# Two of the seven up products made of seven again, with the blocks of x reloaded from DRAM

## The chip, the cores and the metric

The kernel runs on one core of one Trainium2 chip, in one launch. The time is that of the device for one execution, in microseconds (us); the number given for a kernel is the median of its runs. The profile is one further execution, taken by the hardware profiler: it lists the instructions of each engine (PE multiplies matrices, PEld loads its weights, DVE and ACT are the vector and the scalar engine, POOL is GpSimd, SP issues DMAs), when each ran, and what released it when it had waited.

## The reference

An attention without softmax (features from exponentials of a projection) is computed for 8 batches, 8 heads, 576 tokens, 64 wide; its output, as 4608 tokens of 512, goes through a mixture of eight experts, whose shares P come from eight rounds of row and column scaling:

```python
x = np.ascontiguousarray(attn_out.transpose(0, 2, 1, 3)).reshape(B * S, H * D)   # 4608 x 512
...
for e in range(E):                       # E = 8
    h = np.maximum(x @ w1[e], 0.0)       # "up":   512 -> 1024
    ye = h @ w2[e]                       # "down": 1024 -> 512
    out += P[:, e:e + 1] * ye
```

All eight experts are computed for all tokens, so the two matmuls of the loop are most of the work. The inputs come from one fixed draw.

## The kernel before, in words

**Tiles.** x is held transposed in SBUF as bf16, `xT` of 128 partitions x 4 chunks x 4608 tokens. Tokens go in nine groups of 512; groups 0 to 7 are taken in four pairs (1024 tokens), group 8 alone. The results are summed up in fp32 in `acc`, one tile for each group.

**Seven products for eight.** For experts 1 to 7 both matmuls use Winograd's form of Strassen's scheme: each operand is cut into 2 x 2 blocks, sums of blocks are made, and seven block products take the place of eight. The blocks of w1 are added by `sums_up` (L1223), those of w2 by `sums_down` (L1248), those of h inside `down7` (L1468), all on DVE in bf16. The blocks of x are added once, by `sums_x` in expert 1 (L1299): one sum, t1, stands in `xT` in place of a block, three (t2, t3, t4) are stored to DRAM (`Xd`) and loaded again by every later expert (`load_x`, L1317) into the ring `X` of four buffers.

**One unit of work.** `up7` (L1343) makes the seven products of a quarter of the hidden width for a pair: each for two halves q of 128 hidden columns (one PSUM bank each), each half two matmuls of 512 columns (`wide`, L1334, profile line L1338): 28 wide matmuls. The products are called x1, y1, w1, x2, x3, x4, w2. The second (y1, blocks 12 and 21) and the fifth (w1, blocks s1 and t1) are the ones that the change speaks of. What is to be added to two outputs is copied by ACT: x1's bank is copied into y's banks (`move`, L1387) so that y1 accumulates on top of it, x2's into z's, and w1's result goes to SBUF (`keep`, `U`, L1383). Results go to `hs` in bf16 through a Relu, on ACT (`relu`, L1395) where one bank holds the whole sum, or on DVE where the part in `U` has to be added first (`add`, L1390, the ADD_SAT operation that the profile calls CUSTOM_DVE_ANT_0). `down7` makes seven products of one group from such h: 56 matmuls of 256 columns (`product`, L1323, profile line L1329); its results reach `acc` over DVE (`read`, L1522) or over ACT and POOL (`read2`, L1534).

**Loops.** For each expert, for each pair (group 8 last, in expert 7 first), for both quarters fp: one `up7` unit and, interleaved with it, one `down7` of a group whose h is finished. A pair gives two units, group 8 one: nine an expert, in experts 1 to 7. Expert 0 is computed plainly, in and after the attention.

**What sets the order.** Each operation is put into a `Plan` with an engine, an assumed length, what it reads and writes, and buffers. `Plan.schedule` (L261) then plays all engines forward with these lengths: each engine takes the operation that can start first, and among equals the one given first. Each engine's instructions are put out in that order and carry semaphore waits for what they read. The string `ORDER` (L1593) gives the order in which the steps of an up unit (x10 is x1 for half 0) and of a down product set (X1 to Z2) are handed over. Loads of x are issued on SP's queue in the planned order ("order of X"), weights on POOL's. PSUM's eight banks are given out by the class `Banks` (L70): "P1" any bank, "PO" only a bank that a whole-bank matmul started before, since what ACT copies into it is then accumulated on.

Of the kernel before, what the change touches and what calls it, by code (L numbers as in the profile page):

```python
# [17 lines left out]
class Buf:  # L18


    def __init__(self, ring):
        self.ring, self.t, self.slot, self.left, self.end = ring, None, None, 0, 0.0
        self.last = None

# [174 lines left out]
class Plan:  # L199
# [3 lines left out]
    def __init__(self):  # L203
        self.last, self.readers = {}, {}
        self.ops = []
        self.prio = 0
        self.port, self.vector = 0.0, None

    def op(self, eng, dur, lat, fn, r=(), w=(), takes=(), nbytes=0, shared=False):
# [19 lines left out]
        o.bufs = list({id(b): b for b in bufs}.values())  # L229
        for b in o.bufs:  # L230
            b.left += 1
# [12 lines left out]
    def start(self, o, free):  # L244

        t = max(free, o.ready, self.port if o.shared else 0.0)
        if o.eng == "POOL" and o.shared and self.vector:
            t = max(t, self.vector.end)
        need = {}
        for b in o.bufs:  # L250
            if b.slot is None:
                n = need[b.ring] = need.get(b.ring, 0) + 1
                at = b.ring.find(n)
                if at is None:
                    return None
                t = max(t, at)
            elif b.last is not None and b.last.eng != o.eng:
                t = max(t, b.last.end)
        return t

    def schedule(self):  # L261
# [22 lines left out]
        while len(done) < len(self.ops) or links.next():  # L284
# [18 lines left out]
            for b in o.bufs:  # L303
                if b.slot is None:
                    b.slot = b.ring.take(at)
            dur = clock.takes(at, o.dur, o.tiled) if o.eng == "PE" else o.dur
            free[o.eng] = at + dur
# [28 lines left out]
def kernel(  # L336
# [11 lines left out]
    nc = tc.nc  # L348
# [132 lines left out]
    banks = {i: 0.0 for i in range(8)}  # L481
    whole = set()
    for tag, n, kind in (("P1", 1, "whole"), ("P2", 2, "part"), ("PP", 1, "part"),
# [739 lines left out]
    def sums_up(e, w1):  # L1223
# [13 lines left out]
        def k(a):  # L1237
            return [(w1, *a)]
# [4 lines left out]
        sub(dve, 1024, s(3), q(*a12), s(1), ALU.subtract, k(a12) + [S[1]] + late, [S[3]])  # L1243
        return {"11": (q(*a11), k(a11)), "12": (q(*a12), k(a12)), "22": (q(*a22), k(a22)),
                "s1": (q(*a21), k(a21)), "s2": (s(1), [S[1]]), "s3": (s(2), [S[2]]),
                "s4": (s(3), [S[3]])}

# [33 lines left out]
    def xall(gs):  # L1281
        return [k for g in gs for k in xkeys(g)]

    Xd = {(g, n): dram.tile([128, 2, 2, 256], BF16, name=f"xd{g}{n}")
          for g in range(0, NG, 2) for n in (2, 3, 4)}
# [13 lines left out]
    def sums_x(gs, r0=()):  # L1299
# [13 lines left out]
        for n in (3, 2, 4):  # L1313
            move_x(gs, n, True, X)
        return X

# [26 lines left out]
    def up7(A, gs, fp, X, H, r0, inner=()):  # L1343
# [3 lines left out]

        def b(n):
            f, r = {"11": (xq(gs, 0, 1), []), "21": (xq(gs, 1, 1), []), "22": (xq(gs, 1, 0), []),
                    "t1": (xq(gs, 0, 0), []),  # L1350
                    "t2": (lambda: X[2](), [X[2]]), "t3": (lambda: X[3](), [X[3]]),
                    "t4": (lambda: X[4](), [X[4]])}[n]
            return f, r

# [6 lines left out]
        def prod(bank, q, x, y, first, more=(), takes=(), wk=()):  # L1361
            f, r = A[x]
            rhs, r2 = b(y)
            r = xall(gs) + r + r2 + list(more)
            if pair:
# [35 lines left out]
        more = [("banks", i, q) for i in range(2) for q in range(2)]  # L1401
        more += [k for n in ("s2", "s3", "22") for k in A[n][1]] + [X[2]] + list(r0)

# [24 lines left out]
        def w2(q):  # L1428
# [4 lines left out]
            ("x1", x1), ("y1", y1), ("x2", x2), ("w1", w1), ("x3", x3), ("x4", x4), ("w2", w2))  # L1433
            for q in range(2)}

    def acc_part(g, i, j):
# [179 lines left out]
    early, dn = [plain(8)], plain(7)  # L1616
    pairs = [(g, g + 1) for g in range(0, 8, 2)]
    for e in range(1, E):
# [4 lines left out]
        B7 = sums_down(e, w2) if e > 1 else None  # L1623
        turn = [*pairs, (8,)] if e < E - 1 else [(8,), *pairs]
        for n, gs in enumerate(turn):
            X = nextX if e == 1 else load_x(gs)
            H = {g: [] for g in gs}
            for fp in range(len(gs)):
                hs = take()
                for i, z in enumerate(hs):  # L1630
                    H[gs[min(i, len(gs) - 1)]].append(z)
                un = up7(A7, gs, fp, X, H, ["up0"])
                for o in EARLY if e == 1 else ORDER:
                    if len(o) == 3:
# [48 lines left out]
```

## Time and profile before

| | us |
|---|---|
| median of 3 runs | 1022.17 (1021.77 to 1022.48) |
| span of the profiled execution, first to last instruction | 1020.4 |
| what lies around that span, against the median | 1.8 |
| PE busy | 1006.6 |
| DVE busy | 777.5 |
| ACT busy | 743.5 |
| POOL busy | 379.5 |

The profile gives the span and not a time of its own for that execution; the 1.8 us are the difference to the median. A row of a group reads: line, engine, operation, output<-inputs, shapes, count | busy us, mean ns of one | idle time before them and what ended it. Busy time joins rows that overlap. A row of the order in time reads: start, length from the first start to the last end, engine, line, operation, count, and in brackets the idle time ahead of it and its releaser. A matmul's row contains the way of its last result out of the array, so a following matmul starts before it ends; PE's pace is read from starts.

### The profile page before, as it was taken

How to read it: one execution, taken by the hardware profiler on the slowest of the kernel's cores; microseconds unless marked ns; L12 is line 12 of the kernel's file. 1: busy time of each engine (PE TensorE's matmuls, PEld its weight loads, DVE VectorE, ACT ScalarE, POOL GpSimd, SP SyncE). 2: the span in 40 equal slices, each digit the busy share in tenths (PEclk: the TensorE clock that was granted, in tenths of full speed). 3: DMA queues.
4: the chain of work that ended last, by engine and by line, in shares of the span. 5: the costliest groups of instructions: out<-in, count | busy, mean ns of one | idle time of the engine just before them, and what ended most of it. 6: DMA issues, size and time to landing. Idle time of an engine off the chain costs nothing.

```text
span 1020.4 us, 21307 instructions
## 1 busy us (share of the span) xinstructions
PE 1006.6 (99%) x7944; PEld 685.8 (67%) x7944; DVE 777.5 (76%) x1707; ACT 743.5 (73%) x1594; POOL 379.5 (37%) x418
## 2 busy tenths in 40 slices
PE   7899999999999999999999999999999999999998
PEld 5666666644666766676667766676667666776665
DVE  7999989986877777777678767777667767777665
ACT  7999999836988766667666666666666666666663
POOL 5778764400134233322224333422232323333222
PEclk9999999999999999999999999999999999999999
DMA  9999978160013311161116111421125110613333
GB/s 256 181 192 178 183 133 131 38 114 11 32 42 66 86 32 32 27 134 32 31 28 115 31 41 37 80 57 31 32 46 116 32 32 26 119 33 73 133 123 127
DMA packets 107015, 82.85 MB, mean 81 GB/s; under 512 B 53536, under 2 KB 89376, under 8 KB 106912
## 3 DMA queue, kind: packets, MB, share of 16 engines
q1 hardware_dynamic: 74960, 57.44, 22.5%
q0 software_dynamic: 31648, 23.86, 16.4%
q8 instruction: 62, 1.02, 0.4%
q14 instruction: 41, 0.34, 0.1%
q10 hardware_dynamic: 304, 0.20, 0.1%
HBM read 83.18 MB, written 12.98 MB: 94 GB/s over the span
## 4 chain that ended last, share of the span: by engine, by line
PE 95%; DVE 2%; ACT 1%; DMA 1%; issue 0%; POOL 0%; SPq 0%; DVEq 0%; POOLq 0%
PE ps L1329 41%; PE ps L1338 33%; PE ps L603 18%; PE ps L886 2%; DMA v_m<-in_v_dram 1%; ACT q L599 0%; PE ps L733 0%; DVE m L595 0%; DMA acc<-in_k_dram 0%; DVE wx L595 0%; PE ps L915 0%; ACT k L599 0%; ACT wx L599 0%; POOL wx L791 0%; DVE ps L894 0%
## 5 line engine op out<-in xcount | busy, mean ns | idle before, releaser
L1543 POOL TENSOR_TENSOR acc<-acc,hx 128x512 f32<-128x512 f32 x186 | 235.8, 1269 | 563.1 <-DVE hx L1221 310.6
L1329 PEld LDWEIGHTS <-hs 128*128 128x128 bf16 x1984 | 194.1, 98 | 68.9
L1528 DVE SCALAR_TENSOR_TENSOR acc<-ps,P,acc 128x256 f32<-128x256 f32 x372 | 162.8, 479 | 90.3 <-PE ps L1329 83.8
L1391 DVE CUSTOM_DVE_ANT_0 hs<-ps,U 128x512 bf16<-128x512 f32 x252 | 169.3, 688 | 57.2 <-PE ps L1338 41.2
L1388 ACT COPY ps<-ps 128x512 f32<-128x512 f32 x252 | 145.1, 586 | 66.1 <-PE ps L1338 54.0
L1540 ACT ACTIVATE hx<-ps,P 128x256 f32<-128x256 f32 x372 | 156.4, 473 | 46.8 <-PE ps L1329 44.5
L1396 ACT ACTIVATE hs<-ps 128x512 bf16<-128x512 f32 x252 | 151.0, 604 | 43.0 <-PE ps L1338 34.8
L1329 PEld LDWEIGHTS <-hx 128*128 128x128 bf16 x1488 | 145.6, 98 | 38.6
L1338 PE MATMUL ps<-X,T 128*128 128x512 bf16 x448 | 132.8, 379 | 0.0
L1329 PE MATMUL ps<-hx,hs 128*128 128x256 bf16 x992 | 129.1, 273 | 0.0
L1338 PE MATMUL ps<-xT,wx 128*128 128x512 bf16 x384 | 104.3, 379 | 0.0
L1338 PEld LDWEIGHTS <-T 128*128 128x128 bf16 x672 | 65.7, 98 | 48.2
L1559 ACT COPY ps<-ps 128x512 f32<-128x512 f32 x62 | 35.9, 579 | 71.6 <-DVE acc L1528 50.2
L1221 DVE TENSOR_TENSOR hx<-hs 128x512 bf16<-128x512 bf16 x124 | 50.9, 421 | 46.7 <-PE ps L1329 34.6
L1338 PE MATMUL ps<-xT,w 128*128 128x512 bf16 x288 | 77.9, 379 | 0.0
L1384 ACT COPY U<-ps 128x512 f32<-128x512 f32 x126 | 74.9, 594 | 4.0 <-PE ps L1338 3.9
L1338 PEld LDWEIGHTS <-wx 128*128 128x128 bf16 x512 | 50.1, 98 | 40.6
L1329 PE MATMUL ps<-wx,hs 128*128 128x256 bf16 x560 | 76.0, 273 | 0.0
L1338 PE MATMUL ps<-xT,T 128*128 128x512 bf16 x224 | 74.0, 379 | 0.0
L603 PE MATMUL ps<-w,hx 128*128 128x512 bf16 x288 | 72.8, 379 | 0.2 <-ACT q L599 0.2
L603 PE MATMUL ps<-xT,w 128*128 128x512 bf16 x288 | 72.9, 379 | 0.0
L1329 PE MATMUL ps<-wx,hx 128*128 128x256 bf16 x496 | 67.9, 273 | 0.0
(149 smaller groups left out, 1650.2 us busy)
## 6 DMA issues: line engine op xcount, KB each, us to landing
X<-xd SPq DMA_DIRECT2D x72, 256.0 KB, 2.7
wx<-in_moe_w_dram POOLq DMA_DIRECT2D x8, 1024.0 KB, 12.4
v_m<-in_v_dram SPq DMA_DIRECT2D x15, 512.0 KB, 5.7
out_dram<-acc SPq DMA_DIRECT2D x14, 512.0 KB, 2.7
w<-in_moe_w_dram POOLq DMA_DIRECT2D x6, 1024.0 KB, 12.0
qk<-in_k_dram POOLq DMA_DIRECT2D x12, 256.0 KB, 5.7
qk<-in_q_dram POOLq DMA_DIRECT2D x12, 256.0 KB, 6.3
xd<-X SPq DMA_DIRECT2D x12, 256.0 KB, 2.0
```

Source lines behind the costliest of these rows:

```text
L603: nc.tensor.matmul(out_, lhsT=lhsT, rhs=rhs, start=start, stop=stop)
L1221: lambda: f.tensor_tensor(out=out_(), in0=x(), in1=y(), op=op), r, w, **kw)
L1329: pe(256, lambda i=i, k=k, z=z: nc.tensor.matmul(bank()[:, 256 * i:256 * i + 256], lhsT=lhs(k, i), rhs=rhs(k), start=first and z, stop=k = ...
L1338: pe(512, lambda k=k: nc.tensor.matmul(bank().rearrange("p (a b) -> p a b", a=2), lhsT=lhs(k), rhs=rhs(k), start=first and k == 0, stop=k ...
L1384: act(512, lambda: nc.scalar.copy(out=u[q]().rearrange("p a b -> p (a b)"), in_=w[q]()), [w[q]], [u[q]])
L1388: act(512, lambda: nc.scalar.copy(out=to[q](), in_=x[q]()), [x[q]], [to[q]])
L1391: dve(515, lambda: nc.vector._custom_dve(ADD_SAT, out=out_(q, i, j), in0=bank[q]().rearrange("p (a b) -> p a b", a=2), in1=u[q](), s0=3.0e ...
L1396: act(512, lambda: nc.scalar.activation(out=out_(q, i, j), in_=bank[q]().rearrange("p (a b) -> p a b", a=2), func=ACT.Relu, bias=0.0, scal ...
L1528: dve(320, lambda n=n, ts=ts: nc.vector.scalar_tensor_tensor(out=acc[g][:, ts, 256 * j:256 * j + 256], in0=bank()[:, 256 * n:256 * n + 256 ...
L1540: act(370, lambda n=n: nc.scalar.activation(out=u()[:, n, :], in_=bank()[:, 256 * n:256 * n + 256], func=ACT.Copy, bias=0.0, scale=P[:, 4 ...
L1543: pool(695, lambda: nc.gpsimd.tensor_tensor(out=acc[g][:, 2 * i:2 * i + 2, 256 * j:256 * j + 256], in0=acc[g][:, 2 * i:2 * i + 2, 256 * j: ...
L1559: act(512, lambda: nc.scalar.copy(out=y(), in_=x()), [x], [y])
```

## The change

In experts 2 to 7, for pairs, the products two and five are themselves computed from 2 x 2 blocks in seven products. The inner blocks are: of the weights, chunk k by half q; of x, chunk k by group of the pair. One such product was 4 matmuls of 512 columns and becomes 7 matmuls of 256 columns (a new `up49` in place of `up7`). Their sums are made on the way out: ACT copies halves of banks onto each other or into a small buffer `M5`, matmuls accumulate on them, DVE adds `M5` twice. Since the inner product two can't begin on top of x1's copy, x1 is kept in SBUF (`K`) and added by ADD_SAT, where a Relu on ACT stood. The inner sums of the weights are made for each expert by `fine_up`, those of x once, in expert 1, by `fine_x`; they and the plain blocks 11 and 22 are stored to DRAM (`Xi`, `Xp`). From expert 2 on nothing is read from `xT` for the pairs any more: its place holds turning buffers into which `load_fine` loads all seven x operands of a pair (five of 256 KB, two of 448 KB), the weights' inner sums and `M5`. `K` lies where the ring `X` lay. Group 8 keeps `up7`, with its three sums loaded into these buffers. PSUM buffers are now given out nearly in the order in which they were asked for (`inorder`, `seq`), and three new strings `FINE` give the orders: units of pairs, the first unit of an expert's pairs, and group 8.

```diff
-        need = {}
+        need, early = {}, 0
         for b in o.bufs:
             if b.slot is None:
+                if b.seq is not None:
+                    early += b.seq > self.seq + need.get(None, 0)
+                    need[None] = need.get(None, 0) + 1
+                    if early and len(self.banks) - need[None] < 2:
+                        return None
...
+    ring("s_p", [128, 2, 256], FP32, "K", 4)
+    R["K"].make = lambda i: R["X"].make(i).rearrange("p a k c -> p (a k c)").bitcast(
+        FP32).rearrange("p (a c) -> p a c", a=2)
...
+        if e > 1:
+            for n in INNER:
+                fine_up(A, n)
+        return A
+
+    def fine_up(A, n):
+
+        f, r = A[n]
+        t, key, first = FINE_W[n]
+
...
+        def step(n, x, y, op, r, w):
+            sub(dve, 256, s(n), x, y, op, r, [(key, n), *w])
+
+        step(0, a(1, 0), a(1, 1), ALU.add, r, first)
+        step(2, a(0, 0), a(1, 0), ALU.subtract, r, [])
+        step(1, s(0), a(0, 0), ALU.subtract, [*r, (key, 0)], [])
+        step(3, a(0, 1), s(1), ALU.subtract, [*r, (key, 1)], [])
+        A[n + "*"] = t, [(key, i) for i in range(4)]
 
...
+    pairs = [(g, g + 1) for g in range(0, 8, 2)]
+    INNER = {"12": "21", "s1": "t1"}
+    FINE_W = {n: space(3, 1024 * (i + 4 - len(INNER)), 1024, "nfc", (4, 2, 128)) for i, n in enumerate(INNER)}
+    FINE_X = Turns([space(i // 2, 1792 * (i % 2), 1792, "nc", (7, 256)) for i in range(4)])
+    PLAIN_X = Turns([space(2 + i // 4, 1024 * (i % 4), 1024, "akc", (2, 2, 256))
+                     for i in range(5 if len(INNER) > 2 else 6)])
+    M5 = Turns([space(i, 3584, 512, "c", (256,), FP32) for i in range(2)])
...
+    def fine_x(gs, n, b, r0):
+
+        g = gs[0]
+        r = xall(gs) + ["late", *r0]
+        dma("SP", 1 << 16, 160, lambda: nc.sync.dma_start(
+            out=Xi[g, n][:, 0, :], in_=b()[:, 0, 0, :]), r, [("Xi", g, n, 0)])
+        dma("SP", 1 << 17, 160, lambda: nc.sync.dma_start(
+            out=Xi[g, n][:, 1:3, :], in_=b()[:, :, 1, :]), r, [("Xi", g, n, 1)])
...
+        sub(dve, 256, t(0), blk(0, 1), blk(0, 0), ALU.subtract, r, [(y, 0), "order of X"])
+        sub(dve, 256, t(2), blk(1, 1), blk(0, 1), ALU.subtract, r, [(y, 2)])
+        sub(dve, 256, t(1), blk(1, 1), t(0), ALU.subtract, [*r, (y, 0)], [(y, 1)])
+        sub(dve, 256, t(3), blk(1, 0), t(1), ALU.subtract, [*r, (y, 1)], [(y, 3)])
+        dma("SP", 1 << 18, 160, lambda: nc.sync.dma_start(
+            out=Xi[g, n][:, 3:7, :], in_=y().rearrange("p a k c -> p (a k) c")),
+            [(y, i) for i in range(4)], [("Xi", g, n, 2)])
+    def load_fine(gs):
+
+        g, X = gs[0], {}
+
...
+            size = (512 if part else 1024) if turns is PLAIN_X else 1792
+            dma("SP", size << 8, 160, lambda: nc.sync.dma_start(
+                out=t()[:, 0:part] if part else t(), in_=d()), r, [key, *first, "order of X"])
...
+        for n in ("11", "21", "t1", 2, 3, 4, "22"):
+            if n == "22" or n in ("11", "21", "t1") and n not in INNER.values():
+                move(n, lambda n=n: Xp[g, n], [("Xp", g, n, a) for a in range(2)], PLAIN_X)
+            elif isinstance(n, int):
+                move(f"t{n}", lambda n=n: Xd[g, n], [("Xd", g, n)], PLAIN_X)
+            else:
+                move(n, lambda n=n: Xi[g, n], [("Xi", g, n, i) for i in range(3)], FINE_X)
+        return X
...
+        if len(gs) == 2:
+            for n, b in (("22", b22), ("11", b11), ("21", b21), ("t1", b12)):
+                if n in INNER.values():
+                    fine_x(gs, n, b, r0)
+                else:
+                    for a in range(2):
+                        dma("SP", 1 << 17, 160, lambda n=n, a=a, b=b: nc.sync.dma_start(
+                            out=Xp[gs[0], n][:, a], in_=b()[:, a]), r, [("Xp", gs[0], n, a)])
...
+    def up49(A, fp, X, H, gs, r0):
+
+        hb = [H[g][fp] for g in gs]
+        x, y, w = ([new("PO" if n in INNER else "P1"), new("P1")] for n in ("11", "12", "s1"))
+        if "12" not in INNER:
+            y = [new("PO") for _ in range(2)]
+        z = [new("PO") for _ in range(2)]
+        k1 = [new("K") for _ in range(2)]
+        u = [new("U") for _ in range(2)]
+
...
+        def fine(bank, an, xn, more=(), takes=(), wk=()):
+
+            f, r = A[an]
+            s, rs = A[an + "*"]
+            t, rt = X[xn]
+            r = r + rs + rt + list(r0)
+            m5, key, first = M5.next()
...
+            def mul(q, n, lhs, rhs, more=(), takes=(), start=False, wk=()):
+                pe(256, lambda: nc.tensor.matmul(
+                    halves_of(bank[q], n)(), lhsT=lhs(), rhs=t()[:, rhs, :], start=start,
+                    stop=True, skip_group_check=True), r + list(more), [bank[q], *wk], takes)
+
+            def copy(q, n, q2, n2):
+                act(256, lambda: nc.scalar.copy(
+                    out=halves_of(bank[q], n)(), in_=halves_of(bank[q2], n2)()),
+                    [bank[q2]], [bank[q]])
+
+            def a1():
+                mul(1, 0, sf(0), 3, more, takes, True, wk)
+                mul(1, 1, a(0, 0), 0)
+                act(256, lambda: nc.scalar.copy(out=m5(), in_=halves_of(bank[1], 0)()),
+                    [bank[1]], [key, *first])
+                act(256, lambda: nc.scalar.copy(
+                    out=halves_of(bank[0], 0)(), in_=halves_of(bank[1], 1)()),
+                    [bank[1]], [bank[0]])
+
+            def a2():
+                mul(1, 1, sf(1), 4)
+                mul(0, 0, a(0, 1), 1)
+                dve(256, lambda: nc.vector.tensor_tensor(
+                    out=halves_of(bank[0], 1)(), in0=halves_of(bank[1], 1)(), in1=m5(),
+                    op=ALU.add), [bank[1], key], [bank[0]])
+
+            def a3():
+                mul(1, 1, sf(2), 5)
+                mul(0, 1, sf(3), 2)
+                copy(1, 0, 1, 1)
+
+            def a4():
+                mul(1, 0, a(1, 1), 6)
+
+            def last(out_=None, w=None):
+                dve(256, lambda: nc.vector.tensor_tensor(
+                    out=out_() if out_ else halves_of(bank[1], 1)(),
+                    in0=halves_of(bank[1], 1)(), in1=m5(), op=ALU.add),
+                    [bank[1], key] if out_ else [key], [w] if out_ else [bank[1]])
+
+            return a1, a2, a3, a4, last
...
+        own = k1 + u + hb if "12" in INNER else u + hb
+        if "12" in INNER:
+            ys = fine(y, "12", "21")
+        if "s1" in INNER:
+            ws = fine(w, "s1", "t1")
+
+        def x1(q):
+            prod(x, q, "11", "11", takes=own if q == 0 else (), first=True)
+            if "12" in INNER:
+                keep(x, q, k1)
+            else:
...
+        def yk():
+            ys[4]()
+            for q in range(2):
+                add(y, q, k1, 1, 1)
+
+        def wk():
+            keep(w, 0, u)
+            act(256, lambda: nc.scalar.copy(out=u[1]()[:, 0, :], in_=halves_of(w[1], 0)()),
+                [w[1]], [(u[1], 0)])
+            ws[4](lambda: u[1]()[:, 1, :], (u[1], 1))
+
+        def x2(q):
+            prod(x, q, "s2", "t2")
+            act(512, lambda: nc.scalar.copy(out=z[q](), in_=x[q]()), [x[q]], [z[q]])
+
+        def x3(q):
+            prod(x, q, "s3", "t3")
+            add(x, q, u, 0, 0)
+
+        def x4(q):
+            prod(x, q, "22", "t4")
+            relu(x, q, 0, 1)
+
+        def w2(q):
+            prod(z, q, "s4", "22")
+            add(z, q, u, 1, 0)
...
-    ORDER = "X1 x10 w10 x11 X2 x20 y10 x21 Z1 y11 X3 w11 x30 x31 x40 x41 w20 Y1 w21 X4 Z2".split()
     EARLY = ("X1 x10 w10 x11 X2 x20 y10 x21 Z1 y11 X3 w11 x30 x31 x40 x41 w20 Y1 w21 X4 Z2").split()
+    FINE = [("x11 wa wb Z1 x10 wc X1 Z2 wd ya yb X2 wk x20 x21 x30 X3 yc x31 x41 yd x40 w20 Y1 w21 "
+             "yk X4").split(),
+            ("X1 wa ya wb Z1 yb yc wc X2 x11 wd x10 Z2 X3 yd wk X4 x20 x30 x21 yk x31 x41 w20 w21 Y1 "
+             "x40").split(),
+            ("x10 X1 X2 y10 w11 Z1 w10 Y1 x11 X3 x20 x30 x21 X4 Z2 y11 x40 w20 x31 w21 x41").split()]
...
+        if e == 2:
+            o = plan.op("X", 0.0, 0.0, lambda: None, w=["K"])
+            for d in plan.ops[:-1]:
+                if any(b.ring is R["X"] for b in d.bufs):
+                    d.users.append(o)
+                    o.deps.append(d)
+                    o.left += 1
         for n, gs in enumerate(turn):
-            X = nextX if e == 1 else load_x(gs)
+            if (e, n) == (1, 4):
+                plan.inorder = 1
+            X = nextX if e == 1 else load_fine(gs)
...
+                fine = e > 1 and len(gs) == 2
+                if fine:
+                    un = up49(A7, fp, X, H, gs, ["up0", "K"])
+                else:
+                    un = up7(A7, gs, fp, X, H, ["up0"])
+                single = (e, n) >= (1, 4)
+                for o in (FINE[int(fp == 0 and n == (e == E - 1))] if fine else FINE[2] if single else
+                          EARLY):
+                    if o in un:
+                        un[o]()
+                    elif len(o) == 3:
                         un[o[:2], int(o[2])]()
                     elif dn is not None:
                         dn[o]()
```

More of the change, by code (lines that the diff above doesn't have):

```diff
@@ L229, in op @@
         o.bufs = list({id(b): b for b in bufs}.values())
+        if self.inorder:
+            for b in o.bufs:
+                if b.ring.psum and b.seq is None:
+                    b.seq, self.inorder = self.inorder, self.inorder + 1
         for b in o.bufs:
@@ L305, in schedule @@
                     b.slot = b.ring.take(at)
+                    if b.seq is not None:
+                        self.taken.add(b.seq)
+                        while self.seq in self.taken:
+                            self.seq += 1
             dur = clock.takes(at, o.dur, o.tiled) if o.eng == "PE" else o.dur
@@ L1282, in xall, with space, make @@
         return [k for g in gs for k in xkeys(g)]
+    def space(row, at, n, names, dims, dtype=BF16):
+        def make():
+            t = xT[:, row, at:at + n]
+            t = t.bitcast(dtype) if dtype != BF16 else t
+            return t.rearrange(f"p ({' '.join(names)}) -> p {' '.join(names)}",
+                               **dict(zip(names, dims)))
+        first = [k for p in range(at // 1024, (at + n - 1) // 1024 + 1) for k in xall(pairs[p])]
+        return make, ("space", row, at), first
@@ L1363, in prod @@
             rhs, r2 = b(y)
-            r = xall(gs) + r + r2 + list(more)
+            r = (xall(gs) if y not in X else []) + r + r2 + list(more)
             if pair:
@@ L1401, in up7 @@
         more = [("banks", i, q) for i in range(2) for q in range(2)]
-        more += [k for n in ("s2", "s3", "22") for k in A[n][1]] + [X[2]] + list(r0)
+        more += [k for n in ("s2", "s3", "22") for k in A[n][1]] + b("t2")[1] + list(r0)
         def x1(q):
```

112 lines of the change are left out of this document (101 added, 11 removed).

## The prediction

> **What bounds the kernel now.** I read the page's totals and its chain first: they say which engine's time is the kernel's time. The chain of waits comes next, for the length of one turn of the loops, and then the stretches of one expert, for the room that the other engines have.
>
> ```profile
> span 1020.4 us, 21307 instructions
> PE 1006.6 (99%) x7944; PEld 685.8 (67%) x7944; DVE 777.5 (76%) x1707; ACT 743.5 (73%) x1594; POOL 379.5 (37%) x418
> PE 95%; DVE 2%; ACT 1%; DMA 1%; issue 0%; POOL 0%; SPq 0%; DVEq 0%; POOLq 0%
> ```
>
> The chain, around the first pairs of one expert:
>
> ```profile
> 442.41 14.85 PE ps L1329 x136
> ...
> 466.80 2.62 PE ps L1329 x24
> ...
> 491.11 2.62 PE ps L1329 x24
> ...
> 551.89 8.19 PE ps L1329 x75
> ```
>
> The stretches of expert 1 (roughly) and of one later expert; the columns are length, busy time of PE, PEld, DVE, ACT and POOL with instruction counts, granted clock, DMA share and GB/s:
>
> ```profile
> 220.00:332.93 112.93, 112.93 (x687) 66.67 (x686) 85.67 (x190) 88.72 (x172) 23.18 (x19) 1.00 0.15 37
> 442.41:551.89 109.48, 109.48 (x787) 76.69 (x785) 78.82 (x170) 74.14 (x154) 35.85 (x29) 1.00 0.24 53
> ```
>
> The same place returns every 24.31 us (466.80 to 491.11), so one unit, an up product set of a pair's half beside one down product set, takes 12.16 us, and nine make 109.48 us. PE is busy for all of it at full clock; what is taken off PE comes off the time, as long as nothing else keeps PE waiting. DVE has 109.48 - 78.82 = 30.7 us of room in an expert, ACT 35.3.
>
> **What PE saves.** PE in order of time, inside a pair:
>
> ```profile
> 457.10 1.46 PE L1338 MATMUL ps<-xT,wx 128*128 128x512 bf16 x6
> 458.39 1.04 PE L1329 MATMUL ps<-hx 128*128 128x256 bf16 x8
> 459.27 0.59 PE L1338 MATMUL ps<-X,T 128*128 128x512 bf16 x2
> ```
>
> Starts are what counts, since each row's length includes the last result's way out: six wide matmuls take 458.39 - 457.10 = 1.29 us, 0.215 each; eight of 256 columns take 459.27 - 458.39 = 0.88, 0.110 each. (Check: a unit has 28 of the one and 56 of the other, 6.02 + 6.16 = 12.18 us.) A product now is 2 halves x 2 parts = 4 wide matmuls, 0.862 us; made of seven it is 7 narrow ones, 0.767 (7 x 0.1095, the finer division of 0.876 by 8). That is 0.095 us, twice in each fine unit. Fine units: experts 2 to 7, four pairs, two halves = 48. The saving is 96 x 0.0955 = 9.2 us. The narrow pace is the one the down products already keep with a new weight load each (98 ns mean in the page's rows below), so I take no loss for weight loads.
>
> ```profile
> L1329 PEld LDWEIGHTS <-hs 128*128 128x128 bf16 x1984 | 194.1, 98 | 68.9
> L1338 PEld LDWEIGHTS <-T 128*128 128x128 bf16 x672 | 65.7, 98 | 48.2
> ```
>
> **What DVE and ACT are given.** The groups of that expert and how fast such operations follow each other:
>
> ```profile
> L1391 DVE CUSTOM_DVE_ANT_0 hs<-ps,U 128x512 bf16<-128x512 f32 x36 | 24.2, 688 | 9.0 <-PE ps L1338 7.0 <-ACT U L1384 1.0 <-PE ps L1329 1.0
> L1528 DVE SCALAR_TENSOR_TENSOR acc<-ps,P,acc 128x256 f32<-128x256 f32 x54 | 23.6, 479 | 12.8 <-PE ps L1329 12.4 <-ACT hs L1396 0.2
> L1221 DVE TENSOR_TENSOR hs<-hs 128x512 bf16<-128x512 bf16 x18 | 9.2, 523 | 0.1
> L1540 ACT ACTIVATE hx<-ps,P 128x256 f32<-128x256 f32 x55 | 23.1, 470 | 7.3 <-PE ps L1329 6.9
> ```
>
> ```profile
> 462.43 0.42 DVE L1221 TENSOR_TENSOR hx<-hx,hs 128x512 bf16<-128x512 bf16 x1
> 462.76 0.42 DVE L1221 TENSOR_TENSOR hs<-hs 128x512 bf16<-128x512 bf16 x1
> ...
> 464.42 1.29 DVE L1391 CUSTOM_DVE_ANT_0 hs<-ps,U 128x512 bf16<-128x512 f32 x2 [0.26 <-ACT U L1384]
> ...
> 467.71 1.75 DVE L1528 SCALAR_TENSOR_TENSOR acc<-ps,P,acc 128x256 f32<-128x256 f32 x4 [0.18 <-PE ps L1329]
> ```
>
> ```profile
> 459.95 0.57 ACT L1388 COPY ps<-ps 128x512 f32<-128x512 f32 x1 [0.60 <-PE ps L1338]
> ...
> 463.00 0.84 ACT L1540 ACTIVATE hx<-ps,P 128x256 f32<-128x256 f32 x2
> 463.80 0.58 ACT L1384 COPY U<-ps 128x512 f32<-128x512 f32 x1
> ...
> 469.45 0.57 ACT L1559 COPY ps<-ps 128x512 f32<-128x512 f32 x1 [2.15 <-DVE acc L1528]
> 469.94 0.58 ACT L1388 COPY ps<-ps 128x512 f32<-128x512 f32 x1
> ```
>
> A following operation starts before the one ahead has ended, so its price is a pace: ADD_SAT 1.29 - 0.69 = 0.60, the 256-column one from the banks (1.75 - 0.48) / 3 = 0.42, a bf16 sum of 512 0.33 (462.43 to 462.76).
> DVE, per fine unit: product two's result goes out by two ADD_SAT in place of two Relus on ACT, 2 x 0.60 = 1.2. Each fine product has two fp32 additions over 256 columns, four in all. No row has that operation; 0.42 is the upper end, half of ADD_SAT's 0.60 the lower, and I take 0.42, the row of the same shape: 1.7. Together 2.9, so 23.0 in the eight fine units of an expert. The weight sums `fine_up` add 8 bf16 sums of 256, at most 0.33 each: 2.7. Sum 78.8 + 23.0 + 2.7 = 104.5 of an expert that is now 109.48 - 16 x 0.0955 = 107.95 us long: 97% (92% with the lower ends: 78.8 + 19.2 + 1.6 = 99.6). This is the sharp point of the change: DVE does not become the bound by its sum, but its room falls from 30.7 us to between 3 and 8.
> ACT, per fine unit: ten copies or Relus over 512 columns become seven, and seven over 256 come in. At paces of 0.49 (469.45 to 469.94) and 0.37 (0.84 - 0.47): -1.5 + 2.6 = 1.1, 9 us an expert, 74.1 to 83 of 108. It has room.
>
> **New waits on PE.** In a fine product, four groups of PE work hang on each other through one pair of banks: after `a`, ACT must copy two halves out before `b` may add; after `b` DVE must add; after `c` ACT must copy; then `d`. A hop's price if nothing covers it: ACT starts 0.09 us after PE's end (459.27 + 0.59 to 459.95), works 0.47 for one half or 0.37 + 0.47 for two, and the reader behind it starts 0.04 later (463.80 + 0.58 to 464.42): 0.60 and 0.97; over DVE 0.04 + 0.48 + 0.04 = 0.56, plus whatever stands ahead in DVE's queue. The cover is the down product set and the plain up products that the written order puts between: after `wa wb` come `Z1` and `x10`, 0.88 + 0.43 = 1.31 us of PE work. Three hops in each of two products: six a unit, none of them there before. If they are covered, they cost 0; if one of 0.6 is left open in every unit, 48 x 0.6 = 28.8. I take them as covered in the usual order, where the two chains run one after the other, and half of one hop, 0.3, in the six units that open an expert and run both chains at once: 6 x 0.3 = 1.8. The row nearest to this is the stretch above, where PE lost nothing.
>
> **What is moved.** The blocks of x come from DRAM. Three views: the page's list of DMA issues (median us to landing last), the issuing line's own rows (ns, shortest/median/longest) and what SP's queue waited for in this expert (us in total, times, longest):
>
> ```profile
> X<-xd SPq DMA_DIRECT2D x72, 256.0 KB, 2.7
> L1296 SPq DMA_DIRECT2D X<-xd x90: 319/320/373, 332.7 to 975.2; - x90
> SPq L1296 <- PE ps L1338: 91.9, 11, 19.7
> ```
>
> Three loads a pair become seven, two of them of 448 KB: 2.2 MB in 24 us, 91 GB/s where three gave 32. SP's queue issues in 0.32 us, 2.2 of each 24 us; in an expert it now stands waiting for a free place for 91.9 us, so it has the time. t2, t3, t4 and block 22 can only start when the pair before has let go of its place, in the same order in which they are used, half a unit or more ahead against 2.7 us: cost 0; if it failed, up to 2.7 us in each of 24 pairs. In expert 1 each pair stores 12 more pieces and DVE makes 8 more sums (32 x at most 0.33 = 10.7 us on 85.7 of 112.9): hidden. At the turn to expert 2, all first loads wait for expert 1's last readers of x and `K` waits for the last reader of the X ring; group 8's unit (12 us) covers the loads, and X1 and Z1 (1.75 us) the wait: 0. POOL's work is untouched.
>
> **Sum.** -9.2 + 1.8 = -7.4 us. The profiled execution's span is 1020.4, 1.8 below the 1022.17 median, and I take that difference as unchanged: span 1013.0, time **1014.8**. Own range of this case: 1013 (all hops covered) to 1019 (0.1 a unit on top).
>
> **Rivals.** (1) PE waits where it never waited: one open hop a fine unit, because DVE, at 92 to 97%, comes late to its share of the chains or to emptying a bank. It decides from 9.2 / 48 = 0.19 us a unit on; a whole hop of 0.6 gives 1022.2 - 9.2 + 28.8 = 1041.8. For it: the DVE sum. Against: no PE wait at all so far, with some waits of DVE and ACT for PE.
> (2) The hops eat just the saving, 0.15 to 0.23 a unit: 1020 to 1024.
> (3) DVE's operations can't follow each other closely and it becomes the bound. With every operation at its full length an expert needs 36 x 0.688 + 54 x 0.479 + 72 x about 0.445 + 8 x 0.68 + 8 x (2 x 0.688 + 4 x 0.479) + 8 x 0.42 = 118 us, 8.4 more than today: 1022 + 6 x 8.4 = 1073. The paces above speak against it: 1.29 for two ADD_SAT, not 1.38. [...]
> (4) The saving isn't there, as narrow matmuls with strided weights run at 0.123 (0.862 / 7) instead of 0.110: 1022 to 1024. The down products' rows are against it.
> (5) Loads come late: 24 x 1.3 (half of 2.7) gives 1044.
>
> **Chances.** Forecast 0.56, rival 1 0.29, 2 0.08, 3 0.02, 4 0.01, 5 0.04. About 0.2% (2 us) is what a measurement of this kernel can tell from no change: faster 0.56 (the forecast), same 0.09 (2 and 4), slower 0.35 (1, 3 and 5). The range goes from 1011.5 to 1038: below it only an underrated saving, above it rivals 3 and 5 and the worse part of 1.
>
> **What would show it.** Right: an expert of about 108.0 us, PE busy all through, 14 narrow matmuls at 0.11 in each fine unit, DVE at 99 to 105 us of it, no PE wait in the list. Wrong: PE rows that wait for DVE or ACT on the banks, more of them where `wb`, `wc`, `yb`, `yc` stand; a chain of waits with DVE's ADD_SAT and the new 256-column additions in it; or PE waiting for `X` loads at the head of a pair.

## The result and the profile after

The changed kernel takes 1015.93 us (median of four runs, 1015.17 to 1017.20) where the kernel before, run beside it, takes 1022.20 (1021.77 to 1022.48): a ratio of 0.9941, 95% interval 0.9927 to 0.9955. Forecast were 1014.8 us. The profiled execution has a span of 1015.4 us and took 1017.2 in all, the slowest of the four.

First the page of the changed kernel: totals and chain.

```profile
span 1015.4 us, 22728 instructions
PE 996.6 (98%) x8196; PEld 712.8 (70%) x8232; DVE 905.8 (89%) x2075; ACT 765.3 (75%) x1786; POOL 379.8 (37%) x418
PE 92%; DMA 3%; ACT 3%; DVE 1%; issue 1%; POOL 0%; SPq 0%; POOLq 0%; DVEq 0%; ACTq 0%
```

PE is still the bound; its busy time fell by 10.0 us and DVE's rose from 777.5 to 905.8. Now stretches, cut at the same event in both kernels: from the start of the routing sums to the first narrow matmul of group 8 in expert 1, from there to the same matmul in the next expert, and so on, the last one to the end (columns: length, busy time of PE, PEld, DVE, ACT, POOL, clock, DMA share, GB/s). The kernel before, where experts 2 to 6 take 109.48 each, then the changed kernel:

```profile
209.38:334.52 125.14, 125.14 (x754) 72.95 (x754) 95.82 (x216) 93.40 (x180) 24.18 (x20) 1.00 0.24 55
444.00:553.48 109.48, 109.48 (x787) 76.69 (x785) 78.82 (x171) 74.14 (x153) 35.85 (x30) 1.00 0.24 53
881.92:1020.43 138.51, 134.91 (x994) 96.92 (x991) 96.47 (x206) 85.39 (x177) 42.09 (x34) 1.00 0.30 98
```

```profile
211.13:336.45 125.32, 124.66 (x747) 72.71 (x750) 99.47 (x244) 92.90 (x180) 23.43 (x20) 1.00 0.38 98
336.45:445.67 109.22, 108.77 (x838) 81.62 (x836) 100.30 (x228) 79.99 (x189) 35.84 (x30) 1.00 0.38 107
445.67:553.84 108.17, 108.17 (x834) 81.36 (x832) 99.18 (x227) 77.68 (x185) 35.90 (x30) 1.00 0.39 106
553.84:661.92 108.08, 108.08 (x835) 81.38 (x833) 99.10 (x227) 77.68 (x185) 35.92 (x30) 1.00 0.39 107
...
878.14:1015.37 137.23, 133.35 (x1037) 101.33 (x1036) 117.52 (x261) 89.47 (x209) 42.75 (x34) 1.00 0.44 142
```

Read the first column downwards. Against before: +0.2 in expert 1, -0.3 in expert 2, -1.3, -1.4, -1.3 and -1.4 in experts 3 to 6, -1.3 in expert 7: -6.8 us from the cut on. The first cut is not quite the same place, though. PE starts eight matmuls `xT,w` at 207.65 before and at 208.97 after; before, the first routing matmul follows them at 209.38, while in the changed kernel two wide matmuls `w,hx` (0.43 us) come first, at 210.70, and the routing matmul at 211.13. Read from those eight matmuls on, expert 1 costs 0.6 us more, not 0.2, and the kernel is 6.4 us shorter. The attention ahead of them took 1.3 us longer in this execution, so that the span shows only 5.0 of it; the medians differ by 6.3.

All waits of PE from the routing on in the changed kernel (us in total, times, longest) are two, where the kernel before had none:

```profile
PE ps L1462 <- ACT hx L1851: 0.4, 1, 0.4
PE ps L1603 <- DVE ps L1624: 0.4, 1, 0.4
```

And PE in order of time around the two chains of a unit in expert 4:

```profile
597.19 0.27 PE L1603 MATMUL ps<-xT 128*128 128x256 bf16 x1
597.30 0.27 PE L1603 MATMUL ps<-xT,w 128*128 128x256 bf16 x1
597.41 0.49 PE L1462 MATMUL ps<-w,hs 128*128 128x256 bf16 x3
597.74 0.59 PE L1471 MATMUL ps<-xT,T 128*128 128x512 bf16 x2
598.17 1.04 PE L1462 MATMUL ps<-hx,hs 128*128 128x256 bf16 x8
```

The new narrow matmuls (line 1603) keep the old pace: 597.19, 597.30, 597.41. Three more take 0.33, two wide ones 0.43. Between the two matmuls of one group of the chain and the next stand down products and plain up products, and no gap.

### The profile page after: what moved, and what is told of

It reads as the page before. It is cut to its first block, busy times and chain, and to the rows that moved or that the text cites. A ratio compares the mean times of both kernels' runs of the same rounds, so it can differ in the third digit from the quotient of the medians.

```text
span 1015.4 us, 22728 instructions
## 1 busy us (share of the span) xinstructions
PE 996.6 (98%) x8196; PEld 712.8 (70%) x8232; DVE 905.8 (89%) x2075; ACT 765.3 (75%) x1786; POOL 379.8 (37%) x418
## 4 chain that ended last, share of the span: by engine, by line
PE 92%; DMA 3%; ACT 3%; DVE 1%; issue 1%; POOL 0%; SPq 0%; POOLq 0%; DVEq 0%; ACTq 0%
PE ps L1462 41%; PE ps L1471 25%; PE ps L621 16%; PE ps L1603 7%; PE ps L904 2%; DMA rT<-qk_r 1%; DMA v_m<-in_v_dram 1%; DMA xT<-wx 1%; ACT q L617 1%; DMA acc<-in_q_dram 1%; PE ps L751 0%; ACT acc L1861 0%; ACT k L617 0%; DVE m L613 0%; PE ps L933 0%
## 5 line engine op out<-in xcount | busy, mean ns | idle before, releaser
L1471 PE MATMUL ps<-xT,T 128*128 128x512 bf16 x608 | 178.6, 379 | 0.0
L1603 PE MATMUL ps<-xT 128*128 128x256 bf16 x384 | 88.7, 272 | 0.4 <-DVE ps L1624 0.4
L1659 ACT COPY X<-ps 128x512 f32<-128x512 f32 x96 | 56.7, 591 | 24.4 <-PE ps L1471 23.5
L1669 ACT ACTIVATE hs<-ps 128x512 bf16<-128x512 f32 x96 | 56.6, 602 | 22.0 <-PE ps L1471 21.6
L621 PE MATMUL ps<-xT,w 128*128 128x512 bf16 x271 | 70.1, 379 | 0.6
L1721 ACT COPY ps<-ps 128x512 f32<-128x512 f32 x96 | 54.1, 576 | 17.3 <-PE ps L1471 14.9
L1663 DVE CUSTOM_DVE_ANT_0 hs<-ps,X 128x512 bf16<-128x512 f32 x96 | 65.1, 686 | 2.1 <-PE ps L1603 0.8
L1462 PE MATMUL ps<-hx 128*128 128x256 bf16 x496 | 66.3, 272 | 0.0
L1462 PE MATMUL ps<-w,hs 128*128 128x256 bf16 x432 | 65.5, 273 | 0.0
L613 DVE TENSOR_REDUCE m<-ps 128x4 f32<-128x512 f32 x88 | 58.7, 679 | 3.9 <-PE ps L621 1.9
```

The source lines that it names most:

```text
L613: dve(el, lambda: nc.vector.tensor_reduce(out=dst(), in_=src(), axis=AX.X, op=ALU.max, apply_absolute_value=True), r, w)
L621: nc.tensor.matmul(out_, lhsT=lhsT, rhs=rhs, start=start, stop=stop)
L1462: pe(256, lambda i=i, k=k, z=z: nc.tensor.matmul(bank()[:, 256 * i:256 * i + 256], lhsT=lhs(k, i), rhs=rhs(k), start=first and z, stop=k = ...
L1471: pe(512, lambda k=k: nc.tensor.matmul(bank().rearrange("p (a b) -> p a b", a=2), lhsT=lhs(k), rhs=rhs(k), start=first and k == 0, stop=k ...
L1603: pe(256, lambda: nc.tensor.matmul(halves_of(bank[q], n)(), lhsT=lhs(), rhs=t()[:, rhs, :], start=start, stop=True, skip_group_check=True) ...
L1659: act(512, lambda: nc.scalar.copy(out=flat(to[q])(), in_=bank[q]()), [bank[q]], [(to[q], 0), (to[q], 1)])
```

## The experiments

**The theory** was that the gain is the matmul arithmetic alone (0.0955 us for each fine product), that the moved loads give and take nothing, and that the hops of the new chains are free only because the written orders cover them. **Its rivals**: the loads or the new bank rule bring part of the gain; or DVE, at 92% of an expert, is full, so that one thing more would cost its whole length.

**The move alone.** No product is made finer; everything else of the change stays, the seven plain operands of a pair are loaded, and the order is the one of before.

```diff
-    INNER = {"12": "21", "s1": "t1"}
+    INNER = {}
...
-                     for i in range(5 if len(INNER) > 2 else 6)])
+                     for i in range(8)])
...
+    FINE = ["X1 x10 w10 x11 X2 x20 y10 x21 Z1 y11 X3 w11 x30 x31 x40 x41 w20 Y1 w21 X4 Z2".split(),
+            "X1 x10 w10 x11 X2 x20 y10 x21 Z1 y11 X3 w11 x30 x31 x40 x41 w20 Y1 w21 X4 Z2".split(),
+            "X1 x10 w10 x11 X2 x20 y10 x21 Z1 y11 X3 w11 x30 x31 x40 x41 w20 Y1 w21 X4 Z2".split()]
```

> All of the change's moving (blocks of x stored in expert 1, all seven x operands of a pair reloaded into xT's place, PSUM given out in order) but no inner seven: every product is made of four wide matmuls as before, in the order string of before. Theory, the gain is PE work alone: no matmul is saved, so 1022, within 1.5 us of the kernel before; an expert lasts 109.5 us. Rival, part of the gain comes from the moving or the in-order banks: 1016 to 1020. Rival, the reload or its stores cost the 2 to 3 us that are missing from 9.2: 1023.5 to 1025.

1022.98 us, ratio 1.0020 (1.0009 to 1.0031). Two stretches, expert 4 and the last:

```profile
552.88:662.37 109.49, 109.49 (x787) 76.71 (x785) 79.61 (x171) 73.27 (x153) 35.90 (x30) 1.00 0.33 92
881.67:1020.82 139.15, 135.00 (x992) 96.88 (x991) 99.25 (x206) 84.90 (x177) 42.13 (x34) 1.00 0.38 127
```

An expert takes 109.49, as before, while the traffic rose from 53 to 92 GB/s: the move brings nothing, and in a usual expert it costs nothing. The last stretch is 0.6 longer. Its only wait of PE is for a load of x, and the chain that ended last runs through SP's queue (start, length, what):

```profile
934.42 0.29 SPq L1223
...
934.77 0.59 SPq L1223
...
935.40 3.46 DMA xT<-xd
```

In expert 7 group 8 comes first, and its eight output stores stand on SP's queue (in order of time):

```profile
930.32 5.04 SPq L1223 DMA_DIRECT2D out_dram<-acc  x8
```

The load behind them is issued at 935.40, and PE gets it late.

**One product alone.** Only the fifth, as in the diff, then only the second (`{"12": "21"}`), each with an order of its own.

```diff
-    INNER = {"12": "21", "s1": "t1"}
+    INNER = {"s1": "t1"}
```

> Only product five (s1 by t1) is made of seven, product two stays four wide matmuls with Relu on ACT; orders rewritten for it. Theory: 48 x 0.0955 = 4.6 us of matmuls less in all, 0.76 us an expert: an expert of 108.7 us, time 1018 to 1019. DVE gets two 256-column additions a unit and no ADD_SAT more, about 85 us an expert. Rival, hops not covered: no gain over before, 1021 to 1024. Rival, gain not from matmuls: 1015 to 1017.

> Only product two (12 by 21) is made of seven, with x1 kept in SBUF and two ADD_SAT on DVE in place of two Relus on ACT; product five stays as before; orders rewritten for it. Theory: again 4.6 us of matmuls less, an expert of 108.7 us, time 1018 to 1019; the same as with product five alone though DVE has about 9 us an expert more (94). Rival, DVE's load already costs PE something: 1 to 3 us slower than with product five alone.

Five alone: 1019.23, ratio 0.9976 (0.9967 to 0.9986). Two alone: 1020.86, 0.9989 (0.9980 to 0.9999). Expert 4 of the one and of the other:

```profile
552.26:661.05 108.79, 108.79 (x810) 79.04 (x808) 83.45 (x191) 78.43 (x177) 35.82 (x30) 1.00 0.36 99
```

```profile
552.34:661.30 108.96, 108.96 (x810) 79.06 (x809) 92.63 (x207) 72.94 (x161) 35.79 (x29) 1.00 0.36 99
```

Against the move alone an expert loses 0.70 and 0.53; both together lose 1.41. The arithmetic says 8 x 0.0955 = 0.76 for each. So within an expert the saving adds up roughly product by product, as the theory had it. The times do not: both lie above the 1018 to 1019 expected, and product two alone is 1.6 us slower than five alone, as the rival had it. About 0.6 of this lie in experts 2 to 6 together, where DVE has 9.2 us an expert more to do, and 1.0 in expert 7, 0.3 of it in the wait for a load that follows. That DVE's load costs something is therefore not excluded; in expert 4 it is at most 0.17 us. In both, PE waits once for a load behind the same eight stores, 0.8 us with product five and 1.1 with product two. The second case:

```profile
928.69 6.17 SPq L1223 DMA_DIRECT2D out_dram<-acc  x8
934.96 1.02 SPq L1393 DMA_DIRECT2D xT<-xd  x2
```

```profile
937.75 1.02 PE L1471 MATMUL ps<-xT,T 128*128 128x512 bf16 x4 [1.06 <-DMA xT<-xd]
```

The changed kernel itself has its three `xd` loads ahead of the stores (916.37 and 924.39 in its queue) and no such wait.

**The stores on another queue.** The move alone again, with these eight stores issued by ACT.

```diff
-                dma("SP", 1 << 17, 320, lambda b=b, rows=rows: nc.sync.dma_start(
+                dma("ACT", 1 << 17, 320, lambda b=b, rows=rows: nc.scalar.dma_start(
```

> The reload-only kernel e1 with group 8's eight stores to the output issued on ACT's queue in expert 7, not on SP's between the loads of x. If the stores that stand waiting in SP's queue held back the load for which PE waited (0.5 us there, 0.65 by matmul starts), the wait is gone and expert 7's stretch shrinks from 139.15 to about 138.5; the time falls by 0.5 to 0.7 us to about 1022.3, too little for the intervals to tell apart. If the load itself is slow, the wait stays. ACT pays eight issues, which its room covers.

1026.09, ratio 1.0043 (1.0031 to 1.0056): worse than the move alone, where 0.5 to 0.7 us less were expected. The wait for the load is gone, and a longer one has its place (ACT in order of time; then PE's only wait after 700 us):

```profile
930.68 5.06 ACTq L1223 DMA_DIRECT2D out_dram<-acc  x8
935.84 0.57 ACT L1870 COPY ps<-ps 128x512 f32<-128x512 f32 x1 [6.12 <-DMA out_dram<-acc]
```

```profile
PE ps L1462 <- ACT ps L1870: 2.0, 1, 2.0
```

That the stores delay the load is shown by the wait's going; that the 0.2% of the move alone is all of this kind is not, since the edit brought a cost of its own.

**The order.** The changed kernel with each chain written down in one piece (a, b, c, d and the last addition in a row) for the units of pairs.

```diff
-    FINE = [("x11 wa wb Z1 x10 wc X1 Z2 wd ya yb X2 wk x20 x21 x30 X3 yc x31 x41 yd x40 w20 Y1 w21 "
-             "yk X4").split(),
...
+    FINE = ["X1 x10 wa wb wc wd wk x11 X2 x20 ya yb yc yd yk x21 Z1 X3 x30 x31 x40 x41 w20 Y1 w21 X4 Z2".split(),
```

> The changed kernel with the steps of each fine product handed over one right after the other (wa wb wc wd wk, ya yb yc yd yk) within the order of before. Theory, the cover of the hops is the order's doing: four or five of the six hops of 0.6 to 1.0 us in each of 48 units lie open, 1100 to 1200 at the worst, over 1045 in any case. Rival, each engine takes what is ready first and so fills the hops by itself: 1016 to 1022.

1077.54, ratio 1.0543 (1.0508 to 1.0578). The two largest of PE's waits, and expert 4:

```profile
PE ps L1603 <- DVE ps L1624: 7.7, 14, 1.0
PE ps L1462 <- ACT hx L1851: 6.1, 11, 0.8
```

```profile
575.78:693.05 117.27, 112.37 (x835) 81.16 (x833) 97.60 (x227) 78.25 (x185) 35.59 (x30) 1.00 0.35 98
```

The same instructions (835 PE rows, 227 on DVE) take 9.2 us more in an expert, 1.15 in each fine unit: as much as two of the six hops at the forecast's 0.6, where four or five were expected. DVE has no more to do than in the changed kernel. With the work unchanged, the order decides what the hops cost.

**The bank rule.** The changed kernel without `inorder`.

```diff
-                plan.inorder = 1
+                plan.inorder = 0
```

> The changed kernel with one part undone: PSUM buffers are given to whichever step asks first, not nearly in the order of the strings; strings unchanged. Theory, the order of the strings carries the cover only if the banks follow it: steps that are handed over later take banks early, chains wait for banks, PE waits of 0.2 to 0.6 us a unit, 1025 to 1045. Rival, the strings alone carry it: 1015 to 1018.

1034.79, ratio 1.0127 (1.0098 to 1.0157); an expert takes 111.0. The waits of PE:

```profile
PE ps L1603 <- DVE U L1637: 6.5, 12, 0.5
PE ps L1603 <- DVE ps L1624: 2.1, 6, 0.7
```

Narrow matmuls now wait for DVE's last addition in the chain of product five, the only addition that writes `U`. With these strings, the rule that gives banks out in the order asked for is thus a condition of the gain, worth 19 us; strings made without the rule were not tried. No step of the prediction gave it a price.

**More work for DVE.** One ADD_SAT of product two is done twice in each fine unit, to the same result: 0.6 us more on DVE, nothing more on PE. First with the strings as they are, then with strings made for it.

```diff
             for q in range(2):
                 add(y, q, k1, 1, 1)
+            for q in range(1):
+                add(y, q % 2, k1, 1, 1)
```

> The changed kernel with one ADD_SAT of each fine unit done twice (same inputs, same output), 0.60 us more on DVE a unit, 4.8 us an expert: 99.1 becomes about 104 of 108 us; same order strings. Theory by sums (PE bounds until DVE is full): no change, 1016 to 1017.5. Rival 1 of the prediction (DVE late to its share of the chains before it is full): PE waits of 0.1 to 0.6 us a unit, 1021 to 1045, and the waits show on DVE's additions.

> The same doubled ADD_SAT as in e4, but with order strings made anew for this load. If e4's loss of 2.2 us an expert came from DVE being full at 103 of 110 us, new orders can't help: 1025 to 1028. If it came from when DVE's work falls due (lateness, not fullness), new orders win back most of it: PE's gaps under 1 us an expert, time 1018 to 1021.

With the old strings 1027.10, ratio 1.0051 (1.0036 to 1.0066); with new ones 1019.07, 0.9973 (0.9963 to 0.9983). Expert 4 of the one and of the other:

```profile
554.38:664.78 110.40, 109.68 (x835) 81.21 (x833) 103.02 (x235) 77.21 (x185) 35.92 (x30) 1.00 0.37 104
```

```profile
554.34:662.73 108.39, 108.26 (x834) 81.39 (x833) 104.14 (x235) 78.64 (x185) 35.86 (x29) 1.00 0.38 107
```

Both carry the same work. DVE is busy 104.1 of 108.4 us (96%) in the better one, and the expert is only 0.3 longer than the changed kernel's; in the other it loses 2.3, or 0.29 a unit, past the 0.19 from which on the gain is gone. So DVE was not full at 92%: an operation more costs what it makes late, and the order decides that. With the old strings the chain that ended last shows how (start, length, what):

```profile
572.15 0.88 DVE acc L1841 x3
...
573.33 0.42 DVE ps L1624
573.75 0.38 DVE acc L1841
574.14 0.34 DVE hx L1239
574.53 0.36 ACT ps L1617
574.90 0.76 ACT hx L1853 x2
```

After that PE waits 0.38 us at 575.70 for ACT's `hx`: DVE's backlog comes to PE by way of ACT. Most of PE's listed waits are of this kind (1.9 us for `hx`, 0.4 for DVE's additions), and not on DVE's additions, as was expected.

**A third product.** The first product is made of seven too, again with its own strings. Its three chains share two `M5` buffers, so that the sums of two of them mix and this kernel computes something else than the reference; the instructions are those of three fine products.

```diff
-    INNER = {"12": "21", "s1": "t1"}
+    INNER = {"11": "11", "12": "21", "s1": "t1"}
```

> A third product (11 by 11) made of seven as well, with orders made for it. By matmuls alone: 4.6 us less, 1011. By DVE: two 256-column additions more a unit at 0.33 each and four weight sums, 99.1 + 5.3 + 1 = 105 of 106.7 us an expert; and a third pair of banks is held by a chain. Theory (DVE and the banks are at their limit with two): PE waits, 1035 to 1060. Rival (only sums count): 1011 to 1014.

1042.28, ratio 1.0193 (1.0172 to 1.0215). Expert 4, and the first of PE's waits:

```profile
564.55:676.03 111.48, 110.40 (x859) 83.47 (x856) 104.52 (x247) 84.67 (x209) 35.84 (x29) 1.00 0.38 111
```

```profile
PE ps L1462 <- DVE hx L1239: 2.1, 5, 0.9
PE ps L1603 <- ACT ps L1617: 1.3, 6, 0.3
```

PE has 0.76 us less to do in an expert and takes 3.4 more than with two products. DVE's sum, 104.5, is that of the run before, which lost 0.3, so the sum isn't the cause. That three chains in a unit, with two `M5` and the same banks, leave too little between the hops is argued and not shown; which of these it is, and whether a better order exists, stays open.

**The turn to expert 2.** The new sums and stores of x in expert 1 get a later turn, and the first pair of expert 2 and group 8 get strings of their own; the string for the unit that opens an expert is a new one as well.

```diff
+            plan.prio = 300
             for n, b in (("22", b22), ("11", b11), ("21", b21), ("t1", b12)):
...
+            plan.prio = 0
...
-                for o in (FINE[int(fp == 0 and n == (e == E - 1))] if fine else FINE[2] if single else
-                          EARLY):
+                for o in (FINE[3 + fp] if (e, n) == (2, 0) else FINE[int(fp == 0 and n == (e == E - 1))] if
+                          fine else FINE[5 + (e == 1)] if single else EARLY):
```

> The changed kernel with the inner sums of x put behind other work in expert 1 and own orders for group 8 and for the first pair of expert 2: aimed at the 0.8 us that PE waited for ACT in expert 1 and the 0.8 us at the turn to expert 2. Theory: 1 to 1.5 us less than the changed kernel beside it, 1014 to 1015. Rival, these waits are replaced by others: no difference.

> The changed kernel once more, beside the others. If the attention stage's 1.8 us in the first profile (routing began at 211.1 us, in four other kernels with the same attention at 208.6 to 209.4) are that execution's own, routing begins near 209 here and the span is near 1013.5. If they belong to the change, it begins at 211 again.

1015.21 (1014.07 to 1016.17), ratio 0.9928 (0.9913 to 0.9944); the changed kernel, run once more beside it, 1015.94 (1014.73 to 1017.00), 0.9932 (0.9914 to 0.9950). The intervals lie on each other: it isn't shown to be better. Expert 1 took 124.79 instead of 125.32, and PE's listed wait in it is gone. Expert 2 took 109.37 instead of 109.22, but its stretch holds five narrow matmuls more here (x843 against x838, 0.55 us), so by work it lost 0.4 less; expert 4 is the same at 108.07. Expert 7 holds these five less and took 137.7 instead of 137.2: PE now waits 1.03 us there (at 934.50) for a load of x that stands behind group 8's eight stores. So the edit won 0.9 us where it aimed, and a new wait took it back, as the rival had it.

## Why the prediction was right, point by point

**PE's saving: right.** 0.110 for a narrow matmul with new weights held, and the length of an expert came out at 108.08 to 108.17 where 107.95 was worked out. Rival 4 (0.123) is out by the same rows.

**The hops: near in size, by luck, and in other places than given.** The allowance was 1.8 us, half a hop in each of six opening units. Against 16 x 0.0955 = 1.53 an expert, 0.7 are missing in experts 3 to 6 together, 0.25 in expert 7, 1.26 in expert 2, and 0.6 were added in expert 1: 2.8 us. The cut shifts 0.33 between two of them: expert 2's stretch holds three narrow matmuls more than the next ones (x838 against x835), expert 7's three fewer than before. By work, expert 2 lost 0.9 and expert 7 0.6. So the opening units of experts 3 to 6 lose less than half a hop (0.7 over four whole experts), and experts 1 and 2, where the prediction had 0 and 0.3, take over half of all that is lost. That 1.8 came near is luck: it was put in the wrong place. In expert 2 the opening unit has one hop that stays open (PE in order of time):

```profile
357.19 0.38 PE L1603 MATMUL ps<-xT 128*128 128x256 bf16 x2
357.98 0.38 PE L1603 MATMUL ps<-xT 128*128 128x256 bf16 x2 [0.41 <-DVE ps L1624]
```

Two narrow matmuls are 0.22; the next start 0.79 later, 0.57 of it idle: the hop over DVE, priced at 0.56. The prediction looked there for loads and for `K`; neither shows. A second gap of 0.20 follows at 359.05, so this unit has most of the 0.9. "Hidden" was also wrong for the additional sums of expert 1, by 0.6 us: PE waits there once for ACT, in a stretch where DVE is busier by 3.7 us than before (PE in order of time):

```profile
273.92 1.25 PE L1462 MATMUL ps<-wx,hx 128*128 128x256 bf16 x10
275.61 1.03 PE L1462 MATMUL ps<-hx,hs 128*128 128x256 bf16 x8 [0.43 <-ACT hx L1851]
```

Ten narrow matmuls are 1.09; the next start 1.69 later, so 0.60 are lost at this one place. With the sums put behind other work ("The turn to expert 2") the wait is gone and the expert 0.5 us shorter.

**DVE: the lower end was right.** 99.1 us of an expert, where 99.6 to 104.5 stood and 104.5 was taken. The groups of expert 4:

```profile
L1624 DVE TENSOR_TENSOR ps<-ps,xT 128x256 f32<-128x256 f32 x16 | 6.8, 426 | 0.4 <-PE ps L1603 0.3
L1663 DVE CUSTOM_DVE_ANT_0 hs<-ps,U 128x512 bf16<-128x512 f32 x33 | 21.9, 683 | 0.5 <-PE ps L1471 0.3 <-PE ps L1603 0.2
```

```profile
597.75 0.42 DVE L1624 TENSOR_TENSOR ps<-ps,xT 128x256 f32<-128x256 f32 x1
598.08 0.41 DVE L1239 TENSOR_TENSOR hx<-hx,hs 128x512 bf16<-128x512 bf16 x1
...
602.40 1.28 DVE L1663 CUSTOM_DVE_ANT_0 hs<-ps,U 128x512 bf16<-128x512 f32 x2
```

The fp32 addition of 256 lasts 0.426 but is followed after 0.33; 0.42 had been taken from an operation that does more. For 32 of them that is 2.9 of the 5.4 us. The rest fits overlap of the same kind, from having fewer pauses, but is not shown apart: DVE's waits for PE ahead of its `acc` sums fell from 12.4 us to 7.1 an expert.

**Rival 1 was as near as feared.** Its point was 0.19 us a unit. The changed kernel loses 0.05 (2.2 / 48, expert 1 left out); with 0.6 us more for DVE a unit it loses 0.29 and is slower than before; without the bank rule or with the plain order far more. What decided for the forecast is the order, which the argument had only looked at for one place ("after `wa wb` come `Z1` and `x10`"). Its cause was half right: DVE's lateness, as it said, but set by the order and not by how full DVE is.

**Rival 3 is refuted by the stretch itself.** With each of the 227 operations at its full mean length (count times mean, over all groups of that expert) DVE would need 114.9 us, and the expert took 108.1. The Trainium skill, "VectorE: DVE Perf Modes", section "The DRAIN you can't avoid", says that the next operation does not start until the pipe is empty, but also that one that is not held starts earlier. The trace agrees with the second statement: the two ADD_SAT above, of 0.683 us each, take 1.28.

**ACT was overpriced, without effect:** 77.7 us, not 83. **The loads: right for this kernel** (no wait, 107 GB/s), but not at 0 for the move: as the first experiment shows, group 8's stores in the last expert stand in the same queue, which the prediction didn't count. Rival 5 saw the danger in the wrong place, at each pair's head.

**The sum.** Forecast were 1022.17 - 9.2 + 1.8; the stretches give -9.2 + 2.8 = -6.4, the medians -6.3. Why the attention was 1.3 us longer in this profile stays open. In the repeated run the routing starts at 211.01, again late (0.4 us of it the shifted cut), which by its expectation speaks for the change; yet the attention is the same in all changed kernels, and the profiles of six experiments have it at 208.6 to 209.6 and those of four at 210.0 to 210.6. Both profiled executions of the changed kernel were the slowest of their four. In the first, PE waited 1.5 us for one load of the attention (`rT<-qk_r`), a wait that the kernel before doesn't have; in the repeated one this wait is 0.3, so it isn't the whole cause.

## What to carry to other kernels

Fewer matmuls on an engine that is the bound are worth their pace times their number, provided that each new hop to another engine has other matmuls written between. Ask of the second engine not how full it is but what waits for it next: here 0.6 us more of its work in each 12 us cost 0.3 us an expert with an order made for it, and 2.3 without. And when loads are moved to a queue, look at the one stage in which something else stands on that queue.

## What the runs showed of the hardware

Three things were not expected. DVE can be kept busy for 96% of 108 us beside a PE that hardly waits. Copies of half a bank by ACT follow each other faster than the 0.37 us that had been taken from another ACT operation of that shape (ACT in order of time):

```profile
602.06 0.40 ACT L1615 COPY xT<-ps 128x256 f32<-128x256 f32 x1
602.31 0.42 ACT L1617 COPY ps<-ps 128x256 f32<-128x256 f32 x1
602.61 0.60 ACT L1721 COPY ps<-ps 128x512 f32<-128x512 f32 x1
```

They last 0.40 and 0.42 but start 0.25 and 0.30 apart. And eight stores issued by ACT keep it for 5.06 us, 0.63 each, as long as they keep SP's queue (5.04): on SP the load behind them cost PE 0.5 to 1.1 us, on ACT PE waited 2.0 us for the copy behind them.
